# A late second attention, a chunk-wise opening and a one-operation root estimate in a fused linear-attention and SwiGLU kernel

## Chip, cores and metric

One NeuronCore of a Trainium2 chip. The metric is the device time of one execution in microseconds; lower is better. All executions quoted are of the state "fast". "Span" is the length of one profiled execution, 1.7 to 2.2 us shorter than its timed figure. The engines are written as in the profile: PE (TensorE matmuls), PEld (TensorE weight loads), DVE (VectorE), ACT (ScalarE), POOL (GpSimd), SP (SyncE, whose queue issues nearly all transfers).

## The reference, cut to what matters

For each of 8 batches and 8 heads (sequence 576, head dimension 64) a linear attention is computed, normalised per row, and its output goes through a SwiGLU feed-forward of width 1536:

```python
kv  = einsum('bhsd,bhse->bhde', k, v)
out = einsum('bhsd,bhde->bhse', q, kv)
out = out / sqrt(mean(out*out, -1) + 1e-6) * g_norm
x   = out as (4608, 512)                      # 8 batches x 576 rows
xn  = x / sqrt(mean(x*x, -1) + 1e-6) * rms_g
y   = (silu(xn @ w_gate) * (xn @ w_val)) @ w_out
```

The kernel treats each batch as 512 main rows (four chunks of 128) plus 64 tail rows. All eight tails form a ninth group. So there are nine "attentions" and nine "feed-forwards"; a feed-forward is 12 "up" blocks (gate and value, then `silu(gate) * value` into `h_sb`) and a "down" product.

## The kernel before

Each feed-forward runs while the next attention is woven into its slots. `steps` says what is issued after which up block (`j`, or `j - 0.5` between gate and value of block `j`). In the timelines below each engine takes its instructions in the order in which they are issued here. `stage` has four 1 MB buffers, through which q and all weights go from memory to their bf16 copies.

The first attention computes its sums of squares on PE from a transposed product (`oT`, squared by ACT into `sqT`, then `stat_mm`); all others use `sums` on DVE. The row scale then needs a reciprocal root, computed on DVE in `chain_a` and `chain_b`.

```python
def chain_a(self):                                   # [cut]
    nc.vector.tensor_scalar(out=u, in0=self.ssq, scalar1=D * eps, scalar2=None, op0=OP.add)
    nc.vector.reciprocal(out=r, in_=u)
    ...                                              # t, srow, z
    nc.vector.tensor_scalar(out=yi, in0=z.bitcast(I32), scalar1=1, scalar2=-1,
                            op0=OP.arith_shift_right, op1=OP.bitwise_xor)
    nc.vector.tensor_scalar(out=yi, in0=yi, scalar1=float(0x5F3759E0), scalar2=None, op0=OP.add)

# the opening, [cut] to its end
att.oT(1, gps_pool)
Att.kv_of(0, 2, 3)
round_in(0, "v", nc.vector, 6, 7)
round_in(0, "v", nc.scalar, 7, 8)                    # ACT: ahead of the last squares
warm_pe(3)
att.oT(2, vps_pool)
Att.kv_of(0, 3, 4)
att.stat_mm(0)
...

# loads behind the opening
load_kv_main(1, "k"); load_kv_tail(1, "k"); load_w("g", 1); load_w("v", 1); load_q(1)
load_kv_main(1, "v"); load_kv_tail(1, "v")
for j in (0, 2): load_w("g", 2, j, j + 2); load_w("v", 2, j, j + 2)

# first feed-forward, [cut]: second attention in slots 6 to 10, sums on DVE
 6: pieces(1, "v", nc.vector)[2:] + [qT_pe(0), qT_pe(1)],
 7: [..., kv_batch(1, 0), kv_batch(1, 1), ...],
 7.5: [nxt.o(0), nxt.sums(0)], 8.5: [nxt.o(1), nxt.sums(1)], ...

# second feed-forward, [cut]: third attention
at(3, v casts of batch 2);  at(4, kv_batch(2, 0));  at(4.5, kv_batch(2, 1))

# down, from the second feed-forward on: chunk 0 without its last block, then chunk 1, in which
# chunk 0's last block is the fifth product issued
for j in range(NF - 1): self.down_mm(ps, 0, j)
...
if c == 1 and j == 4: self.down_mm(self.first, 0, NF - 1)    # the first reader of h_sb[:, 11]
```

## Time and profile before

| | before |
|---|---|
| median time, first measurement (3 runs) | 330.67 us |
| span of the profiled execution | 328.9 us |
| PE busy | 97% |
| first up matmul / third up block | 23.97 / 27.46 us |
| second feed-forward starts | 59.90 us |
| period of a later feed-forward | 33.23 us |

The page's busy line, the tenths of PE and of the transfers in 40 equal slices of the span (8.2 us each):

```profile
PE 318.6 (97%) x1778; PEld 157.0 (48%) x1778; DVE 184.8 (56%) x413; ACT 181.8 (55%) x325; POOL 16.8 (5%) x31
PE   8789999989999999999999999999999999999995
DMA  8999996999199509930993099929000810050004
```

PE is full, or nearly so, from the fourth slice to the last but one; after the opening a saving must remove a PE gap or PE work, and the transfers are near full through the first six slices and later only in shorter bursts. The PE timeline (start, duration, engine, line, operation, output<-inputs, shapes, count, and in brackets the idle time before it with what ended it), whole lines with others left out:

```profile
23.97 0.60 PE L414 MATMUL g_ps<-xnt,wg_sb 128*128 128x256 bf16 x4
...
27.46 1.03 PE L431 MATMUL g_ps<-xnt,wg_sb 128*128 128x512 bf16 x4
...
39.26 0.44 PE L251 MATMUL att_ps<-v_t,k_t 128*128 128x128 bf16 x5 [0.25 <-POOL v_t L111]
40.18 1.00 PE L251 MATMUL att_ps<-v_t,k_t 128*128 128x128 bf16 x15 [0.48 <-POOL v_t L111]
...
59.90 0.61 PE L414 MATMUL g_ps<-xnt,wg_sb 128*128 128x256 bf16 x4
...
69.59 0.44 PE L251 MATMUL att_ps<-v_t,k_t 128*128 128x128 bf16 x5 [0.84 <-ACT v_t L109]
70.22 0.44 PE L251 MATMUL att_ps<-v_t,k_t 128*128 128x128 bf16 x5 [0.19 <-ACT v_t L109]
...
74.51 0.39 PE L295 MATMUL att_ps<-kv_all,qt 128*128 128x128 bf16 x4
```

L414 is the split up block at the start of a feed-forward, L251 is k·v, L295 is q·kv. The second and the third k·v wait for casts of v (0.73 and 1.03 us). The first ACT cast of v and the last square, from ACT's timeline, and second v's cast, whose start tells when v had landed, from DVE's:

```profile
11.74 0.72 ACT L109 CAST v_t<-kraw_109 128x640 bf16<-128x640 f32 x1 [2.34 <-DMA kraw_109<-in_v_dram]
...
16.98 0.60 ACT L325 ACTIVATE sqT<-v_ps 128x512 bf16<-128x512 f32 x1 [0.85 <-PE v_ps L322]
```

```profile
38.13 1.42 DVE L113 CAST v_t<-kraw_108 128x640 bf16<-128x640 f32 x2 [1.07 <-DMA kraw_108<-in_v_dram]
```

### The profile page before, as it was taken

The page shows a single profiled execution, that of the slowest core. Times are in us where ns is not written, and L with a number is a line of the kernel's source. Part 1 is how long each engine was busy: PE and PEld are TensorE (multiplying, and loading weights), DVE is VectorE, ACT ScalarE, POOL GpSimd, SP SyncE. Part 2 cuts the span into 40 slices and gives each one's busy share as a digit, 9 for nine tenths or more (in the row PEclk, how much of TensorE's full clock was granted, in tenths as well). Part 3 has the DMA queues.
Part 4 walks back from the last instruction along what each step waited for, and adds up shares of the span by engine and source line. Part 5 has one row for each costly group of instructions (what it writes and reads, how often), then busy time and mean ns, then how long its engine had stood idle before and what let it go on. Part 6 is the DMA issues. An engine that isn't in the chain of part 4 may idle for free.

```text
span 328.9 us, 4806 instructions
## 1 busy us (share of the span) xinstructions
PE 318.6 (97%) x1778; PEld 157.0 (48%) x1778; DVE 184.8 (56%) x413; ACT 181.8 (55%) x325; POOL 16.8 (5%) x31
## 2 busy tenths in 40 slices
PE   8789999989999999999999999999999999999995
PEld 3446544645445444544455445544554445444443
DVE  4574889357914890489148913891479137913410
ACT  2575689468574847384748473847272257223321
POOL 2026230000000000000000011000000000000000
PEclk9999999999999999999999999999999999999999
DMA  8999996999199509930993099929000810050004
GB/s 230 321 339 363 321 364 192 266 287 334 56 239 296 138 2 255 313 104 2 250 314 109 0 240 244 236 20 227 28 2 1 214 43 0 0 159 35 0 18 111
DMA packets 78003, 54.84 MB, mean 167 GB/s; under 512 B 45080, under 2 KB 71964, under 8 KB 77980
## 3 DMA queue, kind: packets, MB, share of 16 engines
q1 hardware_dynamic: 73680, 53.88, 58.1%
q0 software_dynamic: 4128, 0.52, 2.4%
q8 instruction: 14, 0.23, 0.3%
q10 hardware_dynamic: 172, 0.13, 0.2%
q14 instruction: 9, 0.07, 0.1%
HBM read 37.75 MB, written 9.44 MB: 143 GB/s over the span
## 4 chain that ended last, share of the span: by engine, by line
PE 80%; DMA 9%; DVE 4%; ACT 2%; SPq 1%; issue 1%; POOL 1%; ACTq 0%; POOLq 0%; DVEq 0%
PE o_ps L446 25%; PE g_ps L431 24%; PE v_ps L439 24%; DMA kraw_108<-in_v_dram 4%; PE att_ps L251 3%; DMA kraw_110<-in_v_dram 2%; DMA kraw_109<-in_v_dram 2%; PE att_ps L295 2%; PE g_ps L446 2%; SPq L87 1%; DVE h_sb L425 1%; DVE xna L379 1%; POOL v_t L111 1%; ACT v_t L109 1%; ACT wg_sb L174 0%
## 5 line engine op out<-in xcount | busy, mean ns | idle before, releaser
L425 DVE TENSOR_TENSOR h_sb<-silu,v_ps 128x512 bf16<-128x512 bf16 x108 | 74.0, 685 | 113.1 <-ACT silu L424 65.4
L439 PE MATMUL v_ps<-xnt,wv_sb 128*128 128x512 bf16 x416 | 106.8, 379 | 0.1
L431 PE MATMUL g_ps<-xnt,wg_sb 128*128 128x512 bf16 x416 | 106.8, 379 | 0.0
L424 ACT ACTIVATE silu<-g_ps 128x512 bf16<-128x512 f32 x108 | 65.2, 604 | 56.9 <-PE g_ps L431 53.7
L446 PE MATMUL o_ps<-wo_sb,h_sb 128*128 128x512 bf16 x396 | 89.3, 379 | 0.1
L446 PEld LDWEIGHTS <-h_sb 128*128 128x128 bf16 x420 | 40.6, 98 | 51.2 <-DVE h_sb L425 2.9
L439 PEld LDWEIGHTS <-wv_sb 128*128 128x128 bf16 x416 | 40.6, 98 | 48.6 <-issue 0.4
L431 PEld LDWEIGHTS <-wg_sb 128*128 128x128 bf16 x416 | 38.9, 98 | 38.9 <-DMA xnt<-xna 0.4
L109 ACT COPY o_sb<-o_ps 128x512 f32<-128x512 f32 x32 | 18.8, 586 | 51.4 <-PE o_ps L446 51.4
L301 ACT ACTIVATE sq<-att_ps 128x512 bf16<-128x512 f32 x32 | 19.2, 600 | 12.0 <-PE att_ps L295 9.2
L109 ACT CAST q_t<-stage 128x512 bf16<-128x512 f32 (+1 forms) x27 | 16.8, 633 | 9.8 <-DMA stage<-in_q_dram 9.8
L316 DVE TENSOR_REDUCE stats<-sq 128x8 f32<-128x512 bf16 x32 | 21.8, 680 | 0.0
L317 DVE TENSOR_REDUCE stats<-wsq 128x8 f32<-128x512 bf16 x32 | 21.7, 677 | 0.0
L379 DVE TENSOR_TENSOR xna<-outa,alpha 128x512 bf16<-128x512 bf16 x32 | 19.9, 685 | 0.1
L306 ACT CAST outa<-att_ps 128x512 bf16<-128x512 f32 x32 | 18.7, 584 | 0.0
L251 PE MATMUL att_ps<-v_t,k_t 128*128 128x128 bf16 x160 | 11.8, 219 | 3.0 <-ACT v_t L109 2.3
L315 DVE TENSOR_TENSOR wsq<-sq,gsq_399 128x512 bf16<-128x512 bf16 x32 | 13.4, 420 | 1.1 <-ACT sq L301 1.1
L251 PEld LDWEIGHTS <-k_t 128*128 128x128 bf16 x160 | 10.3, 97 | 7.6 <-issue 4.2
L295 PEld LDWEIGHTS <-qt 128*128 128x128 bf16 x128 | 9.5, 98 | 6.5
L228 PE MATMUL o_ps<-qt_tail,identity 128*128 128x512 bf16 x34 | 10.8, 473 | 1.4 <-POOL identity masks.py:199 1.4
L295 PE MATMUL att_ps<-kv_all,qt 128*128 128x128 bf16 x112 | 10.8, 219 | 0.0
L141 POOL DMA_DIRECT2D q_t<-in_q_dram x2 | 2.3, 1172 | 148.4 <-DMA qt<-q_t 148.4
(107 smaller groups left out, 173.9 us busy)
## 6 DMA issues: line engine op xcount, KB each, us to landing
stage<-in_q_dram SPq DMA_DIRECT2D x8, 1024.0 KB, 7.5
out_dram<-o_sb SPq DMA_DIRECT2D x16, 512.0 KB, 3.4
kraw_110<-in_k_dram SPq DMA_DIRECT2D x3, 1024.0 KB, 13.0
kraw_108<-in_v_dram SPq DMA_DIRECT2D x3, 1024.0 KB
stage<-in_moe_w_out_dram SPq DMA_DIRECT2D x3, 1024.0 KB, 11.2
stage<-in_moe_w_gate_dram SPq DMA_DIRECT2D x2, 1024.0 KB, 10.3
stage<-in_moe_w_val_dram SPq DMA_DIRECT2D x2, 1024.0 KB, 10.6
kraw_109<-in_k_dram SPq DMA_DIRECT2D x2, 1024.0 KB, 8.8
```

What stands on the lines that cost most here:

```text
L109: engine.copy(out=out, in_=in_)
L251: nc.tensor.matmul(ps[:, j - js[0], :], lhsT=kk[:, c, 2 * j : 2 * j + 2, :], rhs=vv[:, 2 * j : 2 * j + 2, c * D : (c + 1) * D], start=(j = ...
L295: nc.tensor.matmul(ps[:, 2 * j : 2 * j + 2, :], lhsT=a, rhs=b, start=(j == 0 and i == 0), stop=(j == NS - 1 and i == len(terms) - 1),)
L301: nc.scalar.activation(out=self.sq[c], in_=ps, func=ACT.Square)
L316: nc.vector.reduce_sum(out=self.ssq[:, c, :], in_=self.sq[c], axis=AX.X)
L317: nc.vector.reduce_sum(out=self.wssq[:, c, :], in_=wsq, axis=AX.X)
L379: engine.tensor_tensor(out=self.xna[:, c], in0=self.outa[c], in1=self.alpha[:, c, :].to_broadcast([128, H, D]), op=OP.mult,)
L424: nc.scalar.activation(out=silu, in_=g_ps, func=ACT.Silu)
L425: nc.vector.tensor_tensor(out=self.h[:, j, :], in0=silu, in1=v_ps, op=OP.mult)
L431: nc.tensor.matmul(g_ps, lhsT=wg_sb[:, s, j * 128 : (j + 1) * 128], rhs=x[:, :, s, :], start=(s == 0), stop=(s == NS - 1),)
L439: nc.tensor.matmul(v_ps, lhsT=wv_sb[:, s, j * 128 : (j + 1) * 128], rhs=x[:, :, s, :], start=(s == 0), stop=(s == NS - 1),)
L446: nc.tensor.matmul(ps, lhsT=self.h[:, j, c * 128 : (c + 1) * 128], rhs=wo_sb[:, j, :], start=(j == 0), stop=(j == NF - 1),)
```

## The change

Its intent is to shorten the opening and to relieve DVE and ACT in the first feed-forward. (1) In the opening, v's last quarter is cast by DVE, eps is added by an fp32 matmul into the sums' bank, the first weight blocks are loaded in column halves shared out between ACT and POOL, and the first two up blocks start on chunk 0 alone. (2) The integer root estimate is one operation instead of two, everywhere. (3) The second attention moves to the end of the first feed-forward and into its down product, with sums on PE; its k and v load after all gate and value weights. (4) The third attention's v casts and k·v come one slot later.

```diff
@@ loads and opening
-    load_w("g", 0)
-    load_w("v", 0)
+    for j in (0, 2):
+        load_w("g", 0, j, j + 2)
+        load_w("v", 0, j, j + 2)
...
+    round_in(0, "v", nc.vector, 6, 8)
     Att.kv_of(0, 2, 3)
-    round_in(0, "v", nc.vector, 6, 7)
-    round_in(0, "v", nc.scalar, 7, 8)
-    warm_pe(3)
+    warm_pe(2)
+    Att.kv_of(0, 3, 4)
     att.oT(2, vps_pool)
-    Att.kv_of(0, 3, 4)
     att.stat_mm(0)
     att.stat_mm(1)
+    att.oT(3, vps_pool)
     warm_pe(2)
-    att.oT(3, vps_pool)
...
-    round_w12(0, "g", nc.scalar, 2, 4)
-    round_w12(0, "v", nc.gpsimd, 0, 2)
+    round_w12(0, "v", nc.scalar, 0, 2)
+    round_w12(0, "v", nc.gpsimd, 2, 4)
+    round_w12(0, "g", nc.gpsimd, 2, 4)
@@ stat_mm and chain_a
+                nc.tensor.matmul(st_ps, lhsT=ones, rhs=eps_row, start=True, stop=False)
...
-                out=yi, in0=z.bitcast(I32), scalar1=1, scalar2=-1,
-                op0=OP.arith_shift_right, op1=OP.bitwise_xor,
-            )
-            nc.vector.tensor_scalar(out=yi, in0=yi, scalar1=float(0x5F3759E0), ..., op0=OP.add)
+                out=yi, in0=z.bitcast(I32), scalar1=-0.5, scalar2=float(0x5F3759E0), op0=OP.mult, op1=OP.add,
+            )
@@ loads behind the opening
-    load_kv_main(1, "k")
-    load_kv_tail(1, "k")
     load_w("g", 1)
     load_w("v", 1)
     load_q(1)
-    load_kv_main(1, "v")
-    load_kv_tail(1, "v")
-    (second half-blocks of weights)
+    load_w("g", 2)
+    load_w("v", 2)
+    load_kv(1)
@@ first feed-forward and its down, cut
+        9.5: pieces(1, "v", nc.vector)[:2],
+        10: pieces(1, "v", nc.scalar)[2:],
+        11: [..., kv_batch(1, 0), kv_batch(1, 1), nxt.oT(0), nxt.oT(1)],
+        (down) 0: [nxt.oT(2), nxt.oT(3)], 1: [stat_mm(0), stat_mm(1), ...],
+        2: [stat_mm(2), stat_mm(3), chain_a, chain_b, o(0)], ... 5: [o(3), scale, xT_dma, ...]
@@ second feed-forward
-                at(3, (v casts of batch 2))
+                at(4, (v casts of batch 2))
-                at(1 + 3 * late, kv_batch(n + 1, 0)); at(2 + 2.5 * late, kv_batch(n + 1, 1))
+                at(5 if late else 1, kv_batch(n + 1, 0)); at(5.5 if late else 2, kv_batch(n + 1, 1))
```

More of the change, by code (lines that the diff above doesn't have):

```diff
@@ L221 @@
     nc.vector.memset(ones, 1.0)
+    eps_row = consts.tile([1, 2 * T * H], FP32, name="eps_row")
+    nc.vector.memset(eps_row, 0.0)
+    nc.vector.memset(eps_row[:, 0 : T * H], D * eps)
     ident_f = consts.tile([NS, NS], FP32, name="ident_f")
@@ L242, in __init__ @@
             self.xna = None
+            self.with_eps = False
         @staticmethod
@@ L331, in stat_mm @@
                 self.wssq = self.st_ps[:, 1].rearrange("p c j h -> p c (j h)")
+                nc.tensor.matmul(
+                    self.st_ps.rearrange("p u c j h -> p (u c j h)"), lhsT=ones, rhs=eps_row, start=True, stop=False,
+                )
+                self.with_eps = True
             for c in range(T):
@@ L334, in stat_mm @@
                     self.st_ps[:, :, c, j, :], lhsT=self.sqT[:, j, c, :], rhs=sel,
-                    start=(j == 0 and c == 0), stop=(j == NS - 1 and c == T - 1),
+                    start=False, stop=(j == NS - 1 and c == T - 1),
                 )
@@ L341, in chain_a @@
             shape = [128, T, H]
-            u = stat_pool.tile(shape, FP32, name="u")
-            nc.vector.tensor_scalar(out=u, in0=self.ssq, scalar1=D * eps, scalar2=None, op0=OP.add)
+            u = self.ssq
+            if not self.with_eps:
+                u = stat_pool.tile(shape, FP32, name="u")
+                nc.vector.tensor_scalar(out=u, in0=self.ssq, scalar1=D * eps, scalar2=None, op0=OP.add)
             r = stat_pool.tile(shape, FP32, name="r")
@@ L355, in chain_a @@
             nc.vector.tensor_scalar(
-                out=yi, in0=z.bitcast(I32), scalar1=1, scalar2=-1,
-                op0=OP.arith_shift_right, op1=OP.bitwise_xor,
+                out=yi, in0=z.bitcast(I32), scalar1=-0.5, scalar2=float(0x5F3759E0), op0=OP.mult, op1=OP.add,
             )
-            nc.vector.tensor_scalar(out=yi, in0=yi, scalar1=float(0x5F3759E0), scalar2=None, op0=OP.add)
             self.z, self.y = z, yi.bitcast(FP32)
@@ L402, in __init__, with up_parts @@
             self.h = h_pool.tile([128, NF, MAIN], BF16, name="h_sb")
-        def up_halves(self, js):
+        def up_parts(self, js, parts, between=None):
             x = xnts[self.n]
@@ L409, in up_halves @@
             ]
-            for i in range(2):
+            for i, (c0, c1) in enumerate(parts):
                 for j, pair in zip(js, tiles):
@@ L414, in up_halves @@
                             nc.tensor.matmul(
-                                ps[:, i * MAIN // 2 : (i + 1) * MAIN // 2],
-                                lhsT=w_sb[:, s, j * 128 : (j + 1) * 128], rhs=x[:, 2 * i : 2 * i + 2, s, :],
-                                start=(i == 0 and s == 0), stop=(i == 1 and s == NS - 1),
-                            )
+                                ps[:, c0 * 128 : c1 * 128],
+                                lhsT=w_sb[:, s, j * 128 : (j + 1) * 128], rhs=x[:, c0:c1, s, :],
+                                start=(i == 0 and s == 0), stop=(c1 == T and s == NS - 1),
+                            )
+                if between is not None:
+                    between(i)
             for j, (g_ps, v_ps) in zip(js, tiles):
@@ L555 @@
     att.oT(1, gps_pool)
+    round_in(0, "v", nc.vector, 6, 8)
     Att.kv_of(0, 2, 3)
-    round_in(0, "v", nc.vector, 6, 7)
-    round_in(0, "v", nc.scalar, 7, 8)
-    warm_pe(3)
+    warm_pe(2)
+    Att.kv_of(0, 3, 4)
     att.oT(2, vps_pool)
-    Att.kv_of(0, 3, 4)
     att.stat_mm(0)
     att.stat_mm(1)
+    att.oT(3, vps_pool)
     warm_pe(2)
-    att.oT(3, vps_pool)
     att.stat_mm(2)
-    warm_pe(3)
+    warm_pe(2)
     att.stat_mm(3)
     for c in range(T):
-        att.o(c, square=False, pool=(ops_pool, gps_pool)[c // 2], keep=True)
+        att.o(c, square=False, pool=(gps_pool, ops_pool)[c // 2], keep=True)
     warm_pe(12, vps_pool)
     round_w12(0, "g", nc.scalar, 0, 2)
-    round_w12(0, "g", nc.scalar, 2, 4)
-    round_w12(0, "v", nc.gpsimd, 0, 2)
+    round_w12(0, "v", nc.scalar, 0, 2)
+    round_w12(0, "v", nc.gpsimd, 2, 4)
+    round_w12(0, "g", nc.gpsimd, 2, 4)
     att.chain_a()
@@ L578 @@
         att.scale(c, nc.vector)
-    for c in range(T):
-        att.xT_pe(c, nc.scalar, pool=(att_pool, vps_pool)[c // 2])
-    round_w12(0, "v", nc.scalar, 2, 4)
+    for c in range(3):
+        att.xT_pe(c, nc.scalar)
     gsq8 = consts.tile([128, H, D], BF16, name="gsq8")
@@ L594 @@
     load_q(1)
-    load_kv_main(1, "v")
-    load_kv_tail(1, "v")
-    for j in (0, 2):
-        load_w("g", 2, j, j + 2)
-        load_w("v", 2, j, j + 2)
+    load_w("g", 2)
+    load_w("v", 2)
+    load_kv(1)
     def run(steps, slot):
@@ L609 @@
     steps = {
-        1: pieces(1, "k", nc.gpsimd) + [lambda: round_w12(1, "g", nc.gpsimd)] + pieces(1, "v", nc.gpsimd)[:2],
+        1: [lambda: round_w12(1, "g", nc.gpsimd), lambda: load_w("o", 0)],
         2: [lambda: round_w12(1, "v", nc.vector, 0, 2)],
-        4: [lambda: round_w12(1, "v", nc.vector, 2, 4)],
-        5: pieces(1, "q", nc.scalar)[:2] + pieces(1, "q", nc.vector)[2:] + [lambda: load_w("o", 0)],
-        6: pieces(1, "v", nc.vector)[2:] + [lambda: nxt.qT_pe(0, nc.scalar), lambda: nxt.qT_pe(1, nc.vector)],
-        7: [lambda: round_w12(2, "g", nc.scalar, 0, 2), kv_batch(1, 0), kv_batch(1, 1),
-            lambda: round_w12(2, "v", nc.vector, 0, 2), lambda: load_w("o", 1)],
-        7.5: [lambda: nxt.o(0), lambda: nxt.sums(0)],
-        8: [lambda: round_w12(2, "g", nc.scalar, 2, 4), lambda: round_w12(2, "v", nc.gpsimd, 2, 4)],
-        8.5: [lambda: nxt.o(1), lambda: nxt.sums(1)],
-        9: [lambda: load_w("o", 2),
-            lambda: load_kv_main(2, "k"), lambda: load_kv_tail(2, "k")],
-        9.5: [lambda: nxt.o(2), lambda: nxt.sums(2)],
-        10: [lambda: nxt.o(3), lambda: round_wo(0, nc.gpsimd, 0, 2), lambda: nxt.sums(3)],
-        11: [lambda: round_wo(0, nc.scalar, 2, 4)],
-    }
-    ffn.up_halves((0, 1))
+        3: [lambda: round_w12(1, "v", nc.vector, 2, 4)],
+        4: pieces(1, "q", nc.scalar)[:2] + [lambda: load_w("o", 1)],
+        5: pieces(1, "q", nc.vector)[2:] + [lambda: round_w12(2, "g", nc.gpsimd),
+            lambda: round_w12(2, "v", nc.vector, 0, 2)],
+        6: [lambda: round_w12(2, "v", nc.vector, 2, 4), lambda: load_w("o", 2)],
+        7: [lambda: nxt.qT_pe(0, nc.scalar), lambda: nxt.qT_pe(1, nc.vector)] + pieces(1, "k", nc.gpsimd),
+        8: [lambda: load_kv_main(2, "k"), lambda: load_kv_tail(2, "k")],
+        9.5: pieces(1, "v", nc.vector)[:2],
+        10: pieces(1, "v", nc.scalar)[2:],
+        11: [lambda: round_wo(0, nc.scalar, 0, 1), lambda: round_wo(0, nc.gpsimd, 1, 4),
+            kv_batch(1, 0), kv_batch(1, 1), lambda: nxt.oT(0, vps_pool), lambda: nxt.oT(1, vps_pool)],
+    }
+    ffn.up_parts(
+        (0, 1), ((0, 1), (1, 2), (2, 4)), lambda i: att.xT_pe(3, nc.vector) if i == 0 else None,
+    )
     for j in range(NF):
@@ L631 @@
     steps = {
-        0: [nxt.chain_a, nxt.chain_b],
-        1: [lambda: nxt.scale(0, nc.vector), lambda: nxt.scale(1, nc.vector), lambda: nxt.xT_dma(0, 2)],
-        2: [lambda: round_wo(1, nc.scalar), lambda: nxt.scale(2, nc.vector), lambda: nxt.scale(3, nc.vector),
-            lambda: nxt.xT_dma(2, 4)],
-        3: [lambda: load_q(2), lambda: load_kv_main(2, "v"), lambda: load_kv_tail(2, "v")],
-        6: [lambda: round_wo(2, nc.scalar)],
-        8: pieces(2, "k", nc.scalar),
+        0: [lambda: nxt.oT(2, vps_pool), lambda: nxt.oT(3, vps_pool)],
+        1: [lambda: nxt.stat_mm(0), lambda: nxt.stat_mm(1), lambda: round_wo(1, nc.scalar)],
+        2: [lambda: nxt.stat_mm(2), lambda: nxt.stat_mm(3), nxt.chain_a, nxt.chain_b,
+            lambda: nxt.o(0, False, att_pool, True)],
+        3: [lambda: nxt.o(1, False, vps_pool, True)],
+        4: [lambda: nxt.o(2, False, vps_pool, True), lambda: round_wo(2, nc.scalar)],
+        5: [lambda: nxt.o(3, False, att_pool, True), lambda: nxt.scale(0, nc.vector),
+            lambda: nxt.scale(1, nc.vector), lambda: nxt.xT_dma(0, 2), lambda: nxt.scale(2, nc.vector),
+            lambda: nxt.scale(3, nc.vector), lambda: nxt.xT_dma(2, 4)],
+        6: [lambda: load_q(2), lambda: load_kv_main(2, "v"), lambda: load_kv_tail(2, "v")],
+        8: pieces(2, "k", nc.gpsimd),
     }
@@ L660 @@
                 at(2, *pieces(2, "q", nc.scalar)[2:], nxt.qT_dma)
-                at(3, *pieces(2, "v", nc.scalar)[:2], *pieces(2, "v", nc.vector)[2:])
+                at(4, *pieces(2, "v", nc.scalar)[:2], *pieces(2, "v", nc.vector)[2:])
             if not nxt.tail:
-                at(1 + 3 * late, kv_batch(n + 1, 0))
-                at(2 + 2.5 * late, kv_batch(n + 1, 1))
+                at(5 if late else 1, kv_batch(n + 1, 0))
+                at(5.5 if late else 2, kv_batch(n + 1, 1))
             for c in range(T):
@@ L688 @@
                 if unit == 0:
-                    ffn.up_halves((0, 1))
+                    ffn.up_parts((0, 1), ((0, 2), (2, 4)))
             elif unit < NF:
```

## The prediction

> **What bounds the kernel now.** The page's busy line: TensorE 97% of a 328.9 us span. By the table of stretches it is full from 24 us on. Its only gaps after that (timeline): 0.25 + 0.48 us near 39-40 us (second attention, waiting for GpSimd's cast of v), about 0.7 us in crumbs up to 60 us, and 0.84 + 0.19 us at 68.7-70 us (third attention, v landing at 68.7). So only the opening (first feed-forward matmul at 23.97 us) and some 2.5 us of gaps can be saved; a matmul added after 24 us costs its full time.
>
> **The change, part by part.**
>
> 1. Opening. The chain of waits: v landing 11.6 us, casts, k·v, squares (the last 16.98-17.58 us, held up by ScalarE's v piece at 15.15), sums, VectorE chain 17.93-21.1, four scalings (0.62 us each) to 23.68, transposes. Casting v's last quarter on VectorE frees the last squares: -0.9 us. Eps by matmul and the one-op estimate each remove a 0.19 us operation with its gap: -0.44 us. GpSimd's weight cast from 20.10 us coincides with VectorE operations of 0.27 and 0.43 us that take 0.19 elsewhere; the Trainium skill's "SBUF — State Buffer" (Who interferes with whom) says VectorE with two SBUF inputs contends with GpSimd reading SBUF, and the trace agrees. The earlier chain ends before the weights land (~20 us): -0.3 us. Starting on chunk 0 alone gains little more, as 128-column matmuls stream at 0.057 us: two blocks in parts take 3.5-3.6 us as now. Third up block at about 25.5 instead of 27.46 us: **-1.9 us**.
>
> 2. Second attention, TensorE. New: four 512-column matmuls (0.21 us each), 16 sum matmuls (0.025 each; 8 took 0.34 us with one latency), one fp32 eps matmul (0.2): **+1.5 us** on a full engine. VectorE's sums (12 operations, 7.1 us) and the ScalarE copies that go were hidden.
>
> 3. Order of loads. Second k and v come after all gate/value weights. At the present 320-390 GB/s, second v lands near 42 us instead of 38, but is needed only after the last up block (about 43.9), so that stage's present waits go: **-1.4 us**. But loads become just-in-time: the q load waits for GpSimd's half of the first weights (about 24 us), nearly draining the queues; VectorE's v casts sit in order behind the DMA, with two PSUM buffers of slack; the first w_out block lands near 45 us, when down wants it. New gaps: **+0.9 us**.
>
> 4. Third attention. The second feed-forward's transposes finish before down ends (now issued at 56.5 us), so third q and v load earlier, about 65 us, and k·v moves to slot 5: the 1.03 us gap and 0.3 us at the second up's start go: **-1.3 us**.
>
> 5. From the third feed-forward on, TensorE is full and unchanged: 0.
>
> Sum: -1.9 + 1.5 - 1.4 + 0.9 - 1.3 = -2.2 us.
>
> **Prediction: 328.4 us; 326.6 to 330.4 in 8 of 10. Faster by over 2%: 0.03; within: 0.95; slower: 0.02.**
>
> **What would show it.** First up matmul near 21.7 us, third block near 25.5; last square ending near 16.7; second feed-forward starting at 57.7-58.5 instead of 59.9; no TensorE gap near 68; from 70 us the same sequence, shifted by 2-2.5 us. Second v landing near 42 us, TensorE gaps of tenths at 36-46 us.
>
> **What would make it wrong.** Second v or w_out later still: VectorE, blocked behind the DMA, would starve TensorE by 1-3 us at 36-47 us. The first weights' 1 KB pieces landing after 20.5 us, or GpSimd's two casts (1.9 us each) missing 25.5 us. Or smaller new gaps: 327.5.

## The result

Measured: 329.87 us (329.83 to 330.13, 4 runs) after, 330.52 us (329.81 to 331.33, 4 runs) before, on the same chip. The ratio is 0.9981 with a 95% interval of 0.9957 to 1.0005. A ratio here is always the mean time of one kernel's fast runs over the mean of the other's fast runs of the same rounds, so not quite the ratio of the quoted medians. The time lies in the predicted range, but a gain of 2.2 us had been forecast and about 0.6 us came, not clear of the noise. A repeat on another chip gave 330.17 us, ratio 0.9985 (0.9958 to 1.0012).

The profiled span fell by more than the time: from 328.9 to 327.9 us. The time outside the span is 1.7 to 1.9 us in every execution of before, and 2.1 to 2.2 us in every one of after. So some 0.4 us of the gain was lost outside the profiled span, which nobody had predicted. The same 2.1 to 2.2 us show in a1, e2, e3, e6, e8 and x3, the runs that have both the new opening and the late second attention, and in no other run; the reason isn't shown.

The page's lines after:

```profile
PE 317.6 (97%) x1816; PEld 158.7 (48%) x1816; DVE 178.4 (54%) x397; ACT 173.1 (53%) x304; POOL 21.4 (7%) x38
PE   7799979999999999999999999999999999999995
DMA  8999997999399509950994099919000900050004
```

The PE timeline after, at the places shown of before (L425 the split up block, L257 k·v, L328 the transposed product `oT`, L301 q·kv):

```profile
22.29 0.39 PE L425 MATMUL g_ps<-xnt,wg_sb 128*128 128x128 bf16 x4
...
26.11 1.03 PE L444 MATMUL g_ps<-xnt,wg_sb 128*128 128x512 bf16 x4
...
46.01 1.30 PE L257 MATMUL att_ps<-v_t,k_t 128*128 128x128 bf16 x20 [1.38 <-DVE v_t L113]
48.31 0.60 PE L328 MATMUL v_ps<-qt,kv_all 128*128 128x512 bf16 x2 [1.00 <-DVE kv_all L262]
...
61.34 0.60 PE L425 MATMUL g_ps<-xnt,wg_sb 128*128 128x256 bf16 x4
...
71.74 0.72 PE L257 MATMUL att_ps<-v_t,k_t 128*128 128x128 bf16 x10
73.16 0.72 PE L257 MATMUL att_ps<-v_t,k_t 128*128 128x128 bf16 x10
74.58 0.39 PE L301 MATMUL att_ps<-kv_all,qt 128*128 128x128 bf16 x4
```

And the timelines of ACT and of DVE:

```profile
11.74 0.72 ACT L109 CAST v_t<-kraw_109 128x640 bf16<-128x640 f32 x1 [2.73 <-DMA kraw_109<-in_v_dram]
...
16.60 0.60 ACT L331 ACTIVATE sqT<-v_ps 128x512 bf16<-128x512 f32 x1 [0.29 <-PE v_ps L328]
```

```profile
45.37 0.89 DVE L113 CAST v_t<-kraw_108 128x640 bf16<-128x640 f32 x2 [3.40 <-DMA kraw_108<-in_v_dram]
```

First v was cast at 11.74 us in both profiles, so the marks can be compared directly:

| stretch | before | after | difference |
|---|---|---|---|
| start to third up block | 27.46 | 26.11 | -1.35 |
| third block to second feed-forward | 32.44 | 35.23 | +2.79 |
| second feed-forward to third attention's first q·kv | 14.61 | 13.24 | -1.37 |
| from there to the end of the span | 254.4 | 253.3 | -1.1 |

So the third attention gained what was hoped, and the opening some 70% of it (1.35 us of 1.9). The second stage gave more than 2 us back, and a stage that I had called unchanged gained 1 us.

What delays the second stage can be read from the lines: PE finishes the last up block near 44.6 us and waits 1.38 us for second v, which DVE can cast only from 45.37 us. Then it waits another 1.00 us for `kv_all`. ACT's and DVE's lines show what that second wait is: ACT's own casts of v stand in front of the last silu, the last `h_sb` product waits for that silu, and the masking of `kv_all` stands behind it in DVE's order:

```profile
45.35 1.35 ACT L109 CAST v_t<-kraw_108 128x640 bf16<-128x640 f32 x2 [2.68 <-DMA kraw_108<-in_v_dram]
46.61 0.59 ACT L437 ACTIVATE silu<-g_ps 128x512 bf16<-128x512 f32 x1
```

```profile
47.23 0.69 DVE L438 TENSOR_TENSOR h_sb<-silu,v_ps 128x512 bf16<-128x512 bf16 x1 [0.37 <-ACT silu L437]
47.84 0.75 DVE L262 TENSOR_TENSOR kv_all<-att_ps,own 128x256 bf16<-128x256 f32 x2
```

The queue's timeline shows why v is late:

```profile
14.67 1.33 SPq L164 DMA_DIRECT2D stage<-in_moe_w_val_dram  x1
24.37 0.37 SPq L104 DMA_DIRECT2D stage<-in_q_dram  x1
24.90 0.46 SPq L164 DMA_DIRECT2D stage<-in_moe_w_gate_dram  x1
27.07 0.37 SPq L164 DMA_DIRECT2D stage<-in_moe_w_val_dram  x1
...
33.58 4.81 SPq L92 DMA_DIRECT2D kraw_108<-in_v_dram  x1
```

Nothing is issued between 16.0 and 24.37 us. The second q load needs the stage buffer of the first gate block, and half of that block is cast by POOL, which ends near 24.3 us. The transfers fell to 246 GB/s in the stretch from 24 to 26 us, from 392 in the one before.

### The profile page after: what moved, and what is told of

The parts are those of the page before. It is cut to its first block, busy times and chain, and to the rows that moved or that the text cites. A ratio compares the mean times of both kernels' runs of the same rounds, so it can differ in the third digit from the quotient of the medians.

```text
span 327.9 us, 4857 instructions
## 1 busy us (share of the span) xinstructions
PE 317.6 (97%) x1816; PEld 158.7 (48%) x1816; DVE 178.4 (54%) x397; ACT 173.1 (53%) x304; POOL 21.4 (7%) x38
## 4 chain that ended last, share of the span: by engine, by line
PE 87%; DMA 6%; DVE 3%; SPq 1%; ACT 1%; issue 1%; ACTq 0%; DVEq 0%
PE o_ps L459 26%; PE g_ps L444 25%; PE v_ps L452 25%; DMA kraw_108<-in_v_dram 4%; PE att_ps L257 2%; DMA kraw_109<-in_v_dram 2%; PE att_ps L301 2%; PE g_ps L459 2%; PE g_ps L425 1%; PE v_ps L425 1%; DVE h_sb L438 1%; SPq L87 1%; DVE wv_sb L176 1%; DVE xna L389 1%; PE v_ps L328 0%
## 5 line engine op out<-in xcount | busy, mean ns | idle before, releaser
L307 ACT ACTIVATE sq<-att_ps 128x512 bf16<-128x512 f32 x28 | 16.7, 597 | 11.7 <-PE att_ps L301 8.9
L322 DVE TENSOR_REDUCE stats<-sq 128x8 f32<-128x512 bf16 x28 | 19.1, 681 | 0.0
L323 DVE TENSOR_REDUCE stats<-wsq 128x8 f32<-128x512 bf16 x28 | 19.0, 678 | 0.0
L389 DVE TENSOR_TENSOR xna<-outa,alpha 128x512 bf16<-128x512 bf16 x28 | 17.4, 686 | 0.0
L312 ACT CAST outa<-att_ps 128x512 bf16<-128x512 f32 x28 | 16.3, 581 | 0.0
L257 PE MATMUL att_ps<-v_t,k_t 128*128 128x128 bf16 x160 | 11.6, 219 | 2.9 <-ACT v_t L109 1.5
L257 PEld LDWEIGHTS <-k_t 128*128 128x128 bf16 x160 | 10.2, 98 | 7.3 <-issue 3.6
L301 PEld LDWEIGHTS <-qt 128*128 128x128 bf16 x128 | 9.4, 98 | 6.4
L321 DVE TENSOR_TENSOR wsq<-sq,gsq_393 128x512 bf16<-128x512 bf16 x28 | 11.7, 420 | 0.0
L233 PE MATMUL o_ps<-qt_tail,identity 128*128 128x512 bf16 x32 | 9.3, 441 | 1.4 <-POOL identity masks.py:199 1.4
L301 PE MATMUL att_ps<-kv_all,qt 128*128 128x128 bf16 x104 | 10.1, 219 | 0.0
```

The lines of the kernel that those rows point to most:

```text
L257: nc.tensor.matmul(ps[:, j - js[0], :], lhsT=kk[:, c, 2 * j : 2 * j + 2, :], rhs=vv[:, 2 * j : 2 * j + 2, c * D : (c + 1) * D], start=(j = ...
L301: nc.tensor.matmul(ps[:, 2 * j : 2 * j + 2, :], lhsT=a, rhs=b, start=(j == 0 and i == 0), stop=(j == NS - 1 and i == len(terms) - 1),)
L307: nc.scalar.activation(out=self.sq[c], in_=ps, func=ACT.Square)
L322: nc.vector.reduce_sum(out=self.ssq[:, c, :], in_=self.sq[c], axis=AX.X)
L323: nc.vector.reduce_sum(out=self.wssq[:, c, :], in_=wsq, axis=AX.X)
L389: engine.tensor_tensor(out=self.xna[:, c], in0=self.outa[c], in1=self.alpha[:, c, :].to_broadcast([128, H, D]), op=OP.mult,)
```

## The experiments

The expectations name theories by letters. A: the removed DVE operation shortens the late stages. B: the dip in the queues at 24 us makes second v late. C: the second stage is bound by the arrival of its loads, so that the late second attention costs 2.8 us and an earlier opening is waited away. E: the eps matmul holds the last square. F: third k·v stood a slot too early. G: ACT's casts ahead of the last silu make the second wait. H: the two small parts bring the gain, the two large ones take it back.

The table gives the marks of each profile, all counted from the start of the first v cast of that execution. That moment varies from 11.05 to 12.46 us with the arrival of the very first loads, which all these kernels share, and counting from it takes most of this noise out. "v" is the start of second v's first cast, "FF2" the start of the second feed-forward, "period" that of an undisturbed later feed-forward.

| run | ratio to before (95%) | median us | third block | v | FF2 | period |
|---|---|---|---|---|---|---|
| before | 1 | 330.5 | 15.72 | 26.39 | 48.16 | 33.23 |
| after | 0.9981 (0.9957-1.0005) | 329.87 | 14.37 | 33.61 | 49.60 | 33.09 |
| a1 after again | 0.9985 (0.9958-1.0012) | 330.17 | 14.34 | 33.79 | 51.08 | 33.09 |
| e1 one-operation estimate alone | 0.9974 (0.9951-0.9997) | 329.68 | 15.24 | 26.49 | 48.03 | 33.09 |
| e2 after, two operations | 1.0023 (0.9994-1.0053) | 331.22 | 14.61 | 33.12 | 49.11 | 33.23 |
| e3 after, five stage buffers | 0.9967 (0.9937-0.9996) | 329.21 | 14.41 | 32.63 | 48.62 | 33.09 |
| e4 after, old second attention | 0.9943 (0.9917-0.9970) | 328.82 | 14.40 | 26.33 | 47.81 | 33.09 |
| e5 after, old opening | 0.9934 (0.9911-0.9957) | 328.78 | 16.11 | 32.06 | 48.65 | 33.09 |
| x7 e5 again | 0.9959 (0.9930-0.9987) | 329.24 | 17.20 | 32.87 | 49.83 | 33.09 |
| e6 after, squares first | 0.9995 (0.9967-1.0022) | 330.86 | 14.62 | 34.01 | 50.00 | 33.09 |
| e7 third attention alone | 0.9971 (0.9948-0.9994) | 330.03 | 15.78 | 26.25 | 47.99 | 33.23 |
| e8 after, no second tails (wrong result) | 0.9888 (0.9864-0.9912) | 327.53 | 14.36 | 31.02 | 47.23 | 33.09 |
| b2 old second attention, tuned | 1.0160 (1.0138-1.0182) | 336.33 | 14.41 | 26.56 | 52.96 | 33.09 |
| x3 late second attention, tuned | 0.9941 (0.9915-0.9966) | 328.81 | 14.41 | 32.40 | 47.91 | 33.09 |
| x6 two small parts alone | 0.9923 (0.9900-0.9945) | 328.56 | 15.32 | 26.16 | 47.62 | 33.09 |
| x5 mixed | 0.9878 (0.9861-0.9894) | 326.88 | 14.49 | 31.70 | 47.23 | 33.09 |

### e1 and e2: the late stages

```diff
 e1 = before, with the one-operation estimate
 e2 = after, with
-  tensor_scalar(yi, z as int, -0.5, 0x5F3759E0, mult, add)
+  tensor_scalar(yi, z as int, 1, -1, arith_shift_right, bitwise_xor)
+  tensor_scalar(yi, yi, 0x5F3759E0, add)
```

> The kernel before with the one-operation root estimate and nothing else. Theory A (the removed VectorE operation of 0.18 us with its gap delays the last h_sb write in each feed-forward, and TensorE waits for it at the 16th down matmul): every feed-forward from the third on gets 0.14 us shorter (period 33.23 -> 33.09 us), the wait of the weight load for h_sb falls from 2.9 to about 1.6 us in all, and the kernel is 0.9 to 1.2 us faster, 329.4 us, ratio about 0.997. Rival (the chain is hidden behind TensorE in the late stages, as I predicted): only the opening gains, 0.2 us, ratio 0.999 or higher, period unchanged at 33.23 us.

> The kernel after with the old two-operation root estimate. Theory A: the period of the late feed-forwards goes back to 33.23 us and the kernel loses 0.9 to 1.3 us, about 330.9 us, so that without this one line the change would be no faster than before. Rival (something else in the change made the late stages faster): the period stays 33.09 us and at most 0.2 to 0.3 us are lost, about 330.1 us.

Both came out as Theory A says, but for one figure: the list of PEld's waits came to 2.0 us in e1 where 1.6 were expected. The period is 33.09 us wherever the estimate has one operation and 33.23 where it has two, whatever else differs. e1 was 0.26% faster than before. e2 was 0.23% slower than before, where after had been 0.19% faster. They were run at other times. In before, DVE's timeline at the end of the chain and PEld's in the fourth feed-forward's down product show the mechanism:

```profile
151.61 0.18 DVE L359 TENSOR_SCALAR yi<-yi 128x32 int32<-128x32 int32 x1
151.71 0.68 DVE L425 TENSOR_TENSOR h_sb<-silu,v_ps 128x512 bf16<-128x512 bf16 x1
...
153.31 0.68 DVE L425 TENSOR_TENSOR h_sb<-silu,v_ps 128x512 bf16<-128x512 bf16 x1
```

```profile
152.84 0.74 PEld L446 LDWEIGHTS <-h_sb 128*128 128x128 bf16 x4
154.05 0.98 PEld L446 LDWEIGHTS <-h_sb 128*128 128x128 bf16 x6 [0.47 <-DVE h_sb L425]
```

The second L425 line is the last write of `h_sb`. It stands in DVE's order behind the chain and ends at 153.99 us. The weight load that reads it starts at 154.05 after 0.47 us of idling; PEld runs ahead of PE (its first load of this down product is at 150.46 us, the first product at 150.84), so most of that is hidden and 0.14 us reaches PE. One operation less in the chain, 0.18 us and its gap, removes the visible part. DVE's lines of the same feed-forward in after:

```profile
151.12 0.18 DVE L367 TENSOR_SCALAR yi<-z 128x32 int32<-128x32 int32 x1
151.21 0.68 DVE L438 TENSOR_TENSOR h_sb<-silu,v_ps 128x512 bf16<-128x512 bf16 x1
...
152.82 0.68 DVE L438 TENSOR_TENSOR h_sb<-silu,v_ps 128x512 bf16<-128x512 bf16 x1
```

The down product starts at 150.56 us there, 0.28 us earlier than in before (150.84 in the chains of waits), and the last `h_sb` write starts 0.49 us earlier. So it leads by 0.21 us more. The list of PEld's waits behind 74 us has six such waits in before, 2.9 us in all, and six of 1.6 us in after. The list is no measure of the gain by itself: x5 and x6 have 2.6 us in it at the same period of 33.09. On PE it comes to 0.93 us from the second down product to the ninth in after (worked out in point 5 of the section on the prediction), and to 0.67 us in e1 (230.44 to 229.77).

### e7: the third attention by itself

```diff
 e7 = before, with
-  at(3, v casts)   at(4, kv_batch 0)   at(4.5, kv_batch 1)
+  at(4, v casts)   at(5, kv_batch 0)   at(5.5, kv_batch 1)
```

> The kernel before with only the third attention's later slots (v casts at 4, k.v at 5 and 5.5); loads as before. Theory F (the 1.03 us wait at 69 us in before was k.v standing one slot too early for the landing of v, so that moving it is enough): the wait goes, everything after it comes 0.8 to 1.1 us earlier, period of the late feed-forwards unchanged at 33.23 us, time 329.7 us, ratio about 0.997. Rival (the wait goes only because the second attention's new order brings the third v earlier): the wait stays or moves to the new slot, time within 0.3 us of before.

Theory F holds: third k·v waits for nothing, and from the second feed-forward to the third attention's first q·kv it is 13.51 us (59.48 to 72.99) instead of 14.61. The time fell by 0.29%. So the later slots alone give 1.10 of the 1.37 us. The other 0.27 us, by the timelines, is a wait of PE for ACT in e7, where a silu stands behind the casts of the third q; in after that q comes earlier and the wait is gone. In the profiled execution of e7, 0.86 us of the gain is lost again between the second down product and the ninth, where the earlier periods vary from run to run.

### e4 and e5: the two large parts undone, one at a time

```diff
 e4 = after, with the loads, slots and DVE sums of before for the second attention
 e5 = after, with the opening of before (casts, order of matmuls, whole weight blocks, two halves)
```

> The kernel after with the second attention and the order of loads of before; the new opening, the eps matmul in the opening, the one-operation estimate and the later slots of the third attention stay. Theory C (the late second attention with its load order costs 2.8 us between the third up block and the second feed-forward): the second feed-forward starts at 58.5 to 59.9 us instead of 61.34, depending on how much of the opening's 1.35 us is lost again to waiting for second v, which lands at 38 us as before; the time is 326.9 to 328.3 us, faster than both kernels. Rival (the late second attention is what brings the third attention's gain and it was worth its cost): the time is 329.9 us or more.

> The kernel after with the opening of before (order of casts and matmuls, weights in whole blocks, first two blocks in two halves); second attention, load order, slots and the one-operation estimate stay. Theory C (in the kernel after, the second stage ends when second v and w_out have landed, so that an earlier opening is only waited away): the third block comes 1.2 to 1.5 us later than in after, but the wait before the second k.v shrinks by about that much, the second feed-forward starts within 0.4 us of after's, and the time is within 0.5 us of after. Rival (the opening's gain is carried through): second feed-forward and end 1.3 us later than after.

Both medians are lower than that of after, though e4's interval overlaps after's. e4 does what Theory C expected at FF2, at the weak end of it: of the opening's 1.3 us only 0.35 us are left there (47.81 against 48.16). Little of the rest is the wait for v, which grew only from 0.73 to 0.85 us; most of it goes at a gate block whose weights POOL casts late (from its first product at 29.24 us it takes 2.08 us instead of 0.86). The time, 328.82 us, missed the expected 326.9 to 328.3. e5 went further than Theory C. It expected to equal after and was better, with FF2 0.95 us earlier where at most 0.4 were expected: v came at 32.06 instead of 33.61, because its gate block is freed by ACT and q is issued at 21.28 us instead of 24.37; there was no wait before k·v. Its third block came 1.74 us later than in after (expected 1.2 to 1.5). Its repeat x7 gave 0.9959, between what I had set as confirming (up to 0.995) and as refuting (0.997). The intervals of the two runs (0.9911 to 0.9957, 0.9930 to 0.9987) meet those of after only at their edges or overlap a little.

The result of every execution also lists its mean granted clock, and this clears up most of the spread. Two executions of a1 and two of x7 have 0.988 to 0.995; those of after and e5 and the others of a1 and x7 have 0.997 or more. Among the latter the eight of after and a1 lie at 329.71 to 330.26 us (mean 329.94), the ten of e5 and x7 at 328.04 to 329.63 (mean 328.86), and the ratios to before become 0.9981 and 0.9970 against 0.9934 and 0.9937. So, by this selection, the new opening *harms* the kernel after, by about 1 us, of which 0.4 us is the time outside the span. The selection was made afterwards, and the calls used different chips.

> The run with the opening undone, unchanged, again on this chip: base for the mixed run and check of its 0.9934. Expected 328.8 us, ratio 0.992 to 0.995; if it comes out at 0.997 or higher, the claim that the new opening harms the kernel after falls.

In x7's profiled execution, one of its two with a lower mean clock, the granted clock was 0.65 in the stretch from 14 to 16 us and 0.50 from 16 to 18 us, which put its third block 1.1 us behind that of e5.

### e8 and e3: what decides the arrival of second v

```diff
 e8 = after, with (wrong on purpose)
-    load_kv(1)
+    load_kv_main(1, "k"); load_kv_main(1, "v")       # tail rows zero or old
 e3 = after, with
-    stage_pool bufs=4
+    stage_pool bufs=5
```

> Wrong on purpose in the second batch: the kernel after, but the two tail loads of the second attention (128 KB each, in pieces of 256 bytes) are left out and the tail rows are zeros or old data. Theory C, measured directly: second v lands 1.5 to 2.5 us earlier (0.26 MB less and the slow stretch of 250 to 310 GB/s at 36 to 40 us gone), TensorE's wait for it goes to under 0.3 us, the second feed-forward starts 1 to 1.5 us earlier and the kernel is 1 to 1.5 us faster than after, about 328.6 us. Rival (the wait is made by VectorE's and ScalarE's casts and their order, not by the arrival): the wait stays above 1 us and the time within 0.4 us of after.

> The kernel after with five staging buffers instead of four, so that the second q load need not wait for GpSimd's half of the first weights (24.3 us). Theory B (the dip of the queues at 24 to 28 us is part of why second v lands at 45.35 us): the dip goes, v lands about 1 us earlier, the TensorE wait before the second k.v shrinks from 1.4 us to 0.4 us or less, the second feed-forward starts near 60.3 instead of 61.34 us, and the kernel is about 1 us faster than after, 328.9 us. Rival (the queues have enough elsewhere and v is late only because of its place at the end of the order): v lands within 0.3 us of 45.35 and the time stays at 329.9 us.

e8 gave a wrong result as intended, and the direct proof. v came 2.6 us earlier (31.02 against 33.61), and both of PE's waits went, not only the one for v:

```profile
43.93 1.28 PE L257 MATMUL att_ps<-v_t,k_t 128*128 128x128 bf16 x20
45.28 0.60 PE L328 MATMUL v_ps<-qt,kv_all 128*128 128x512 bf16 x2
```

Here k·v and `oT` have no bracket: no idle time before them. FF2 came 2.4 us earlier than in after and the time fell to 327.53 us, about 2.6 us under the repeat of after. I had expected only 1 to 1.5 us, as I had overlooked the second wait. It is a consequence of the first, by the lines of ACT and DVE shown with the result. From the third block to FF2 it takes 32.87 us in e8, against 35.23 in after: the two waits (1.38 + 1.00 us) make the whole difference. The Trainium skill's "DMA: Bandwidth & Descriptors" (Why small descriptors are slow) says that pieces of 256 bytes from memory carry a fixed cost each; the runs agree, in kind: 0.26 MB of such pieces cost 2.6 us, of which 0.7 us would be their bytes at 370 GB/s (estimated from the rates around them).

e3 took away the dip in the queues (365 GB/s in the stretch from 24 to 26 us instead of 246). v came 1.0 us earlier relative to first v, as Theory B says, and the wait for it shrank from 1.38 to 0.55 us, where at most 0.4 had been expected. The second wait stayed at 1.00 us. By the ratios the time fell by 0.5 to 0.6 us relative to after (0.9967 against 0.9981 and 0.9985), but the intervals overlap. They were run at other times.

### e6: the order of products in the opening

```diff
 e6 = after, with
     att.oT(2, vps_pool)
+    att.oT(3, vps_pool)
     att.stat_mm(0)        # with the eps matmul in front
     att.stat_mm(1)
-    att.oT(3, vps_pool)
```

> The kernel after with the last transposed product of the opening issued ahead of the eps matmul and the first eight sum matmuls. Theory E (the fp32 eps matmul, 0.36 us in TensorE's order between the third and the fourth product, is what held the last square at 17.20 us instead of my 16.7): the last square ends 0.3 to 0.45 us earlier relative to the landing of first v, the first up block starts 0.3 to 0.45 us earlier; the whole time hardly moves (0 to 0.4 us), since by Theory C the second stage waits for its loads. Rival (ScalarE or VectorE hold it): under 0.1 us.

Half a miss. The last square ended 5.10 us after the first v cast instead of 5.46, as expected, but DVE's chain began 0.31 us *later* (6.21 against 5.90): the eps matmul and the sum matmuls had only been moved behind. So the fp32 eps matmul, 0.36 us in PE's order, does hold up the opening, but so do the sums and warm-up matmuls around it; the squares are not the limit. Removing eps from PE altogether, as in b2 and x3 below, started the chain at 5.77 to 5.78, a gain of 0.13 us, less than the DVE operation that it brings back.

### a1: the kernel after again, and the clock

> The kernel after once more, unchanged, as the base for the other runs of this call, and to see how far the landing of second v (45.35 us in the first profile; 44.1 us in the run with the two-operation estimate, which has the same schedule) varies from run to run. Expected 329.9 us, ratio 0.998, v landing between 44 and 45.4 us, second feed-forward between 60.1 and 61.4 us.

Its time and v were as expected, FF2 was not: 62.68 us against 60.1 to 61.4. The table of stretches (length, then busy time and count of each engine, granted clock, transfers' share, GB/s) shows why:

```profile
44.00:46.00 2.00, 0.59 (x3) 0.09 (x1) 0.60 (x2) 0.61 (x1) 0.00 (x0) 1.00 1.05 367
46.00:48.00 2.00, 1.30 (x20) 1.16 (x20) 1.62 (x4) 1.38 (x4) 0.10 (x1) 0.92 1.05 390
48.00:50.00 2.00, 1.46 (x3) 0.58 (x5) 0.62 (x2) 1.48 (x3) 1.69 (x3) 0.50 1.04 384
50.00:52.00 2.00, 1.97 (x7) 0.84 (x7) 0.00 (x0) 0.67 (x3) 0.00 (x0) 0.73 1.06 365
```

The granted clock fell to 0.50 at 47.68 us, within PE's second wait (47.35 to 48.35 us), and stayed there for about 3.4 us (worked out from 0.92, 0.50 and 0.73). The Trainium skill's "TensorE: Matmul & The Clock Gate" (What's actually happening) describes this: the clock is gated by free-running windows of 3.4 us; an idle one halves it, a busy one restores it. The trace agrees in length, but the window that ended at 47.68 us was not idle: PE was busy for 1.63 us of its 3.41. The start of the down product took 1.3 us longer for it. In the first profile of after the same waits fell otherwise: its windows end at 45.74 and 49.16 us, PE was busy for 2.29 and 2.15 us of them, and the clock stayed at 1.00. So a wait that is only 1.4 + 1.0 us can cost 1.3 us more in some executions; the six times of a1 lie around 330 us (four) and 331.5 us (two). The mean clock says that those two were such executions: 0.995 and 0.992, against 0.998 or more in the four.

### b2 and x3: two attempts at the best of both

```diff
 b2 = e4, without the eps matmul, last oT first; second gate block cast ahead of k on POOL; and
   (down, first feed-forward)
+  0: [load_q(2), load_kv_main(2, "v"), load_kv_tail(2, "v"), chain_a, chain_b],
-  3: [load_q(2), load_kv_main(2, "v"), load_kv_tail(2, "v")],   # behind the transposes
 x3 = e3, without the eps matmul, last oT first; second v's casts behind the last silu (slot 11)
```

> A candidate for the fastest: after with the second attention and load order of before (as e4), and besides: no eps matmul in the opening (the add on VectorE again) with the last transposed product ahead of the sum matmuls, the second gate block cast ahead of k on GpSimd, and the third q and v loads issued ahead of the second feed-forward's transposes instead of behind them. If the eps matmul's place in TensorE's order was the cost in the run with the products first (sums ended 0.35 us later there although the squares ended 0.35 us earlier), VectorE's chain now starts 5.3 to 5.5 us after the first v cast instead of 5.9, and with its extra 0.22 us operation the first up block comes 0.1 to 0.4 us earlier than in after; the waits for GpSimd's gate weights (1 us and more in e4) go; third q lands before 64 us and ScalarE's wait for it goes. Second feed-forward at 58.0 to 58.8 us, time 327.0 to 328.2 us, ratio about 0.990.

> The other candidate: after with five staging buffers, the opening without the eps matmul as in the other run, and the second v casts put behind the last silu and the last h_sb product instead of ahead of them. Theory G (the 1.0 us wait for kv_all behind the wait for v in after was ScalarE's casts standing ahead of the last silu): with v landing near 44 us the wait for kv_all falls below 0.6 us, while the wait for v itself may grow to 1 to 1.5 us; second feed-forward at 59.4 to 60.0 us, time 328.0 to 329.0 us, ratio 0.993 to 0.996. If the second v's landing alone decides (Theory C), it is no faster than the five-buffer run, 0.9967.

b2 was 1.6% slower than before, a plain mistake of mine. The loads put ahead of the transposes kept the queue busy:

```profile
49.81 3.65 SPq L87 DMA_DIRECT2D kraw<-in_v_dram  x1
53.50 2.85 SPq L92 DMA_DIRECT2D kraw<-in_v_dram  x1
56.73 6.82 SPq L399 DMA_TRANSPOSE xnt<-xna  x2
```

```profile
64.67 1.03 PE L421 MATMUL g_ps<-xnt,wg_sb 128*128 128x256 bf16 x4 [4.46 <-DMA xnt<-xna]
```

The issue of the two transposes took 6.82 us instead of 2.69, and PE idled 4.46 us for them. The granted clock then stood at 0.50 from 63.7 to 70.5 us, which is part of the loss. The long issue agrees with the skill's "DMA: Bandwidth & Descriptors" (Queues, rings and completion order): each DMA engine takes the descriptors of one ring in order. x3 came in at 0.9941. Theory G is supported: the wait for `kv_all` was gone, and the wait for v 1.34 us, as expected. Its distance to e3 (0.9967) is within the intervals. They were run at other times.

### x6 and x5: the small parts alone, and the large parts reconciled

```diff
 x6 = before, with the edits of e1 and e7, nothing else
 x5 = e5, with five stage buffers, no eps matmul, and in the opening
+  round_in(0, "v", nc.vector, 6, 8)
   kv_of(0, 2, 3); warm_pe(2); kv_of(0, 3, 4); oT(2); oT(3); stat_mm(0); stat_mm(1); stat_mm(2)
-  (the same with v's last quarter on DVE and ACT, eps, and 8 warm-up matmuls)
```

> The kernel before with the one-operation estimate and the third attention's later slots, nothing else: neither the new opening nor the late second attention. Theory H (these two small parts give all of the change's gain, and the two large parts together take some of it back): about 0.9 + 0.9 us faster than before, 328.9 to 329.2 us, ratio 0.994 to 0.9955, so faster than the kernel after by 1 us or more. Rival (the parts overlap and the large ones are needed for the gain): 329.8 us or more, ratio 0.997 or higher.

> A candidate for the fastest: the late second attention with the opening of before and whole weight blocks (as in the run with the opening undone), plus five staging buffers, v's last quarter cast on VectorE and no eps matmul. Theory H (the late second attention has some slack for v when the weights are cast as in before, so a part of the opening's gain can be kept): third block 0.5 to 0.9 us earlier than in before relative to the first v, v lands 32 us or less after the first v cast, waits before the second k.v under 0.3 us, second feed-forward at 59.3 to 60.0 us, time 327.7 to 328.6 us, ratio 0.990 to 0.9935. Rival (v's landing stays where it is and the gain is waited away): equal to the run with the opening undone within 0.3 us.

x6, with two edits of a few lines, is 0.77% faster than before, and its interval (0.9900 to 0.9945) lies clear below both intervals of after. So the two small parts give more than the whole change, and the two large ones together take it back. x5 is the fastest kernel found, correct, 326.88 us: 1.22% faster than before and below the interval of any other correct run. Its PE timeline in the second stage:

```profile
43.77 1.28 PE L256 MATMUL att_ps<-v_t,k_t 128*128 128x128 bf16 x20
45.78 0.61 PE L327 MATMUL v_ps<-qt,kv_all 128*128 128x512 bf16 x2 [0.72 <-DVE kv_all L261]
```

q is issued at 13.05 us there, v's cast begins 31.70 us after the first, and k·v does not wait; `oT` still waits 0.72 us for `kv_all`. Its opening, with whole weight blocks, no eps matmul and no chunk-wise start, is as fast as that of after (14.49 against 14.37). Against x7 (0.9959) it is clear of noise, and 1.42 us of the 1.62 us by which its third block leads that of e5 are still there at FF2. This agrees with the reading that a faster opening pays once the loads behind it come earlier too, but it is no clean test of it: x5 was planned as a combination, and does not tell how much each of its three edits gives.

## Why the prediction was wrong

Point by point, with the prediction's own terms:

1. **Opening, -1.9: measured -1.35.** The chain's parts were right (last square earlier, one operation less, no collision with POOL's cast at 20 us): DVE's chain up to the first scaling shortened from 3.27 to 2.48 us, as forecast. But the square ended at 17.20 us (-0.38 where -0.9 was forecast); the eps matmul and the sums stand in PE's order before the last product. The chunk-wise start made the first two blocks take 3.82 instead of 3.49 us, where "3.5-3.6" had been forecast; a transpose of 0.22 us falls between its parts.
2. **Second attention on PE, +1.5: not measured by itself.** It is part of the +2.79 of the second stage. An estimate from e8, which has all this work and no such waits: of the +2.79 us, 2.36 are the two waits, and 0.43 is left for the added work less the waits of before that went, forecast as +1.5 - 1.4.
3. **Order of loads, -1.4 + 0.9: the step that failed.** It is the term "New gaps: +0.9", which measured 2.4 us (1.38 for v and 1.00 for `kv_all`; e8 takes both away). I put second v at 42 us by counting the bytes ahead of it at the rates of before. It was cast at 45.37. I had named the late q load and "nearly draining the queues", but given it no time (e3: 1.0 us), and had ignored that the tails come last and slow (e8: 2.6 us with both). I had also sized the wait for v alone, and not the second wait that late v causes through ACT's and DVE's order, nor the clock. Together the stage cost +2.79 us (1.3 more in a1), where the terms for it summed to +1.0. "VectorE, blocked behind the DMA, would starve TensorE by 1-3 us" stood under what would make me wrong, and it is what happened; the mistake is the size.
4. **Third attention, -1.3: measured -1.37, right in size.** The later slots alone give 1.10 us (e7), the earlier loads the other 0.27. The 0.3 us at the second up's start went as forecast, but it lies in the stretch before, and the transposes were not issued earlier (56.66 us against 56.49).
5. **"From the third feed-forward on, TensorE is full and unchanged: 0": measured -0.93.** From the second down product (84.03 and 84.11 us) to the ninth (314.47 and 313.62) it is 230.44 us before and 229.51 after. I took "full" from slices of the span, in which 0.14 us of 33 do not show, although the list of waits in before had 2.9 us of weight loads waiting for `h_sb`. e1 and e2 settle this.

The errors have opposite signs: the opening and the second stage lost more than forecast, the late stages gained what nobody had forecast. That the time still fell in the predicted range is luck. As a forecast of the gain it was wrong: 2.2 us against 0.6.

What stays open: why the time outside the span grew by 0.4 us, how the 0.43 us of the second stage split between added PE work and the waits of before that went, and what each edit of x5 gives alone.

## What to carry to other kernels

A shorter stage in front of one that waits for transfers gained little or nothing here until the transfers were issued earlier too: look at what each load's buffer waits for, and count the bytes and small pieces ahead. "Hidden" work on an engine that executes in order delays everything behind it: find the last write that the busy engine needs and see how much slack it has before calling a chain free. Test the parts of a bundled change one at a time: here two edits of a few lines were worth more than the bundle.

## What the Trainium skill lacked or had wrong

- "TensorE: Matmul & The Clock Gate" (What's actually happening) speaks of an idle window of about 3.4 us and gives no share of activity at which the clock falls; its section on a second failure mode tells of a clock that oscillates where PE idles briefly and often, again without a share. Here windows in which PE was busy for 1.63 us of 3.41 (a1, until 47.68 us) and for 0.99 (x7, until 14.60) were followed by half the clock, windows with 1.68 (x3, until 13.87) and 1.71 us (e6, until 47.22) were not; where a window starts is reckoned from the clock's steps in the same trace, which lie multiples of 3.413 us apart. So the limit lay near half a window, an estimate, as the ends of matmuls are modelled in the traces.
- "DMA: Bandwidth & Descriptors" (DMA Transpose) does not say that transposes wait behind plain loads of their own queue; it follows only from its section on rings. In b2 two transposes took 6.82 us to issue behind 2.2 MB of loads, against 2.69 us in after.
- "DMA: Bandwidth & Descriptors" (Why small descriptors are slow) puts the overhead of 256-byte pieces at 27%. Leaving out 0.26 MB of them (e8) brought v 2.6 us earlier, where their bytes alone come to 0.7 us. No run tells how much of the rest is the size of the pieces and how much that they reach only 64 partitions or come last.
- "SBUF — State Buffer" (Who interferes with whom) agrees with the runs where it was used, but overlap alone does not tell when it bites: a DVE product with two SBUF inputs took 0.57 us in after at 22.5 us, beside POOL's weight cast, and 0.28 us in before at 23.6 us without one; yet in e6 it took 0.28 us at 22.76 us with the cast running beside it (22.38 to 24.30).
